# Three fused blocks on one core: another order of the chunks in the first expert pass, and another end of the last chunk

## The chip, the cores and the metric

One Trainium2 chip, one of its cores. The metric is device time in microseconds (us). The kernel before takes 1118.63 us, the median of three runs (1117.74 to 1119.43).

## The reference

```python
def _attn_ref(q, k, v, phi):            # batch 4, 8 heads, 576 positions, head 64; phi gives 32 memory slots
    a = exp(phi - max(phi, axis=2)); a = a / (sum(a, axis=2) + 1e-09)
    k_m = einsum('bhsm,bhsd->bhmd', a, k)
    v_m = einsum('bhsm,bhsd->bhmd', a, v)
    attn = softmax(q @ k_m.T / sqrt(64))
    return attn @ v_m

def _moe_ref(x, w_in, w_out):           # x 2304 x 512, w_in 512 x 2048
    h = x @ w_in
    g = h * clip(h + 3, 0, 6) / 6
    return g @ w_out

def _moe2_ref(x, domain_probs, w1, w2): # 4 experts, w1 512 x 1024 and w2 1024 x 512 each
    p = domain_probs / (domain_probs.sum(-1, keepdims=True) + 1e-09)
    out = 0
    for e in range(4):
        h = maximum(x @ w1[e], 0)
        out += p[:, e:e+1] * (h @ w2[e])
    return out
```

`reference()` runs the three blocks one behind the other, all in float32; the output is 2304 x 512.

## The kernel before, in words

The kernel has two halves, each laid out by its own planner (class `Plan`): every operation gets an engine, an estimated cost and its dependencies, the planner puts them in an order per engine, and each engine then works its list strictly in that order. TensorE's order in the second half is not the planner's: `t_order` writes it out, and `before` chains each TensorE operation to the one ahead.

The first half (up to about 394 us) does the attention, the gated block and, beside them, part of the work on the expert weights. The second half does the experts. It is cut into **three passes** over 768 tokens each (two halves of TW = 384), and each pass into **eight chunks** of 512 of the experts' 4096 inner columns: chunk n belongs to expert n // 2. A place in this sequence of 24 is called g, so g // 8 is the pass and, before the change, g % 8 the chunk.

A chunk is done with fast matrix multiplication by blocks: seven products instead of eight. At its start stand 14 product groups (`prod`, L910: seven products for each of two units u), which end in the PSUM tiles pa, pb, pd; then come 14 down groups (`down`, L979: seven results k in the order `DOWN` = 1, 5, 7, 6, 2, 4, 3, two halves j each), which end in po. Each group is six matmuls of 128x128 by 128x384, since every operand is split into a high and a low part and three of the four combinations are computed. So a chunk is 28 groups of six on TensorE, with no other work there. The products of a chunk pass through VectorE (t, s: L937, L946, L951) and are split into h (ScalarE L955 the high part, VectorE L959 the low one) for the down groups. The first two products of a chunk are put ahead of the down groups of the chunk before it (`hoist`).

The down results are summed in SBUF over the eight chunks. In the first pass nearly every po bank is **seeded**: ScalarE copies the running sum into the bank (L971), TensorE adds onto it, ScalarE copies it back (L985). Where a group is not seeded, VectorE adds po to the sum (L987). At a pass's last chunk the seven sums are combined into the four output blocks by VectorE (`total`, L990: named u2s, u3s, u4s, c2 to c5 after what they make) and stored (L995). C21 is sum 4.

**The weights.** Every chunk needs 14 weight tiles of 512 KB, called ring tiles (j = 0 to 6 for the products, 7 to 13 for the down groups), in a ring of ten slots, so a slot is free for a new tile when the tile ten back has been used for the last time. A ring tile holds the block sums that the fast multiplication wants, split into high and low parts. For chunks 0 to 4 (`NPRE` = 5) these tiles are made in the first half and stored in DRAM (`ready`). Chunks 5, 6 and 7 are **made on the spot** in the first pass: raw weights are loaded (praw, L372 and L414, three buffers), VectorE forms the sums (L393, L433), ScalarE and VectorE split them into the ring slot (L382 and L385 for the products' tiles, L422 and L425 for the down tiles), and SyncE's queue (SP) stores each tile to DRAM (L388, L428) for passes two and three. All other chunks are read from DRAM by one DMA for each tile (`ring_load`, L895). All DMAs stand in SP's one queue, in order.

The shares of the experts (share, L899: the factors p, 384 KB for one expert and pass, two buffers) are loaded once for each expert and pass.

The planner takes a VectorE operation of 384 columns as 468 ns and a ScalarE copy as 381 ns:

```python
    MM6 = 1041
    V1, A1, C1 = 468, 415, 381
    hoist = lambda g: 0 < g < NG
```

Of the kernel before, what the change touches and what calls it, by code (L numbers as in the profile page):

```python
# [22 lines left out]
E, FF2 = 4, 1024  # L23
# [14 lines left out]
NRAW, NST = 3, 6  # L38
NPRE = 5
GSEED = (0,1,2)  # L40
SEED = ((4, 0), (4, 1), (1, 0), (5, 0), (5, 1), (7, 0), (7, 1), (6, 0), (2, 0), (3, 0))
# [42 lines left out]
class Plan:  # L84
# [9 lines left out]
    def op(self, key, eng, cost, fn, *deps, banks=()):  # L94

        self.ops[key] = eng, cost, fn, deps, banks
# [64 lines left out]
def body(ctx: ExitStack, tc: tile.TileContext, phiT, kv, qT, w_in, w_out, w1, w2, dp, out):  # L161
# [719 lines left out]
    def ring_tile(g, j):  # L881
        if (g, j) not in ring:
            ring[g, j] = slot(RING[place[g, j] % len(RING)], [P, 1024], f"ring{g}_{j}")
        return ring[g, j]

    def jraw_tile(shape, name):
        t = edge_tile(len(jraws) % 3, name)
        jraws.append(t)
        a, b = shape[1:]
        return t.rearrange("p (a f) -> p a f", a=a)  # L890

    def ring_load(i):
        g, j = seq[i]
        ring_tile(g, j)
        nc.sync.dma_start(out=ring[g, j].bitcast(F32), in_=ready[g % NCE][j])  # L895

    def share_load(p, e):
        shr[p, e] = ppool.tile([P, 2, TW], F32, tag="share", name=f"share{p}_{e}")
        nc.sync.dma_start(out=shr[p, e].rearrange("p a t -> p (a t)"),  # L899
                          in_=shared[e, p * 2 * TW:(p + 1) * 2 * TW].partition_broadcast(P))  # L900
# [38 lines left out]
    def scaled(name, half, g, u):  # L939
        s = shr[divmod(g // 2, E)][:, half]  # L940
# [66 lines left out]
    for g in range(NG):  # L1007
# [20 lines left out]
    def freed(i):  # L1028
        if i < len(RING):
            return []  # L1030
        g, j = seq[i - len(RING)]
        return [("pr", g, *LAST[j]) if j < 7 else ("dn", g, DOWN[j - 7], 1), *(stored(g, j) if NPRE <= g < NCE else [])]

    def fetched(g, j, h=None):
        if not NPRE <= g < NCE:
            return [("rl", place[g, j])]
        if j >= 7:
            return [("jv", g, 2, DOWN[j - 7])]
        return [("jv", g, *x) for x, y in UP.items() if y == j and (j != 4 or x[0] == h)]

    def plan_experts():
        loads = []
        for i, (g, j) in enumerate(seq):
            if not NPRE <= g < NCE:
                deps = freed(i)
                if g >= NCE and g % NCE >= NPRE:
                    deps += stored(g % NCE, j)
                op(("rl", i), "Q", 1450, partial(ring_load, i), *loads[-1:], *deps)
                loads.append(("rl", i))
        prev, raws = [], []  # L1050
        for n in range(NPRE, NCE):

# [5 lines left out]
            def part(key, w, hi, lo, store, *deps):  # L1058
                u, k = key
                i = place[n, 7 + DOWN.index(k) if u == 2 else UP[u, k]]  # L1060
# [4 lines left out]
            prepare(n, load, part, op, partial(prep_unit, raw_tile=jraw_tile, place_tile=ring_tile),  # L1065
                    partial(prep_down, raw_tile=jraw_tile, place_tile=ring_tile), "jp", "jl", "jv")
        for p in range(NP):
            for e in range(E):
                n = p * E + e
                op(("sh", p, e), "Q", 1450, partial(share_load, p, e), *([("v", 4 * n - 5, "m12")] if n > 1 else []))  # L1070
        for g in range(NG):
            p, n = divmod(g, NCE)
            share = ("sh", *divmod(g // 2, E))
            for u in range(2):
# [30 lines left out]
            for i, k in enumerate(DOWN):  # L1105
                for j in range(2):
# [19 lines left out]
            if last:  # L1126
# [24 lines left out]

    sd, jraws = [], []
    plan_experts()
# [34 lines left out]
```

## Time and profile before

| | |
|---|---|
| median of three runs | 1118.63 us (1117.74 to 1119.43) |
| the profiled execution: its own time | 1117.6 us |
| its span, from the first to the last instruction | 1115.8 us |
| TensorE (PE) busy | 1087.0 us, 97% |
| VectorE (DVE) busy | 854.7 us, 77% |
| ScalarE (ACT) busy | 757.8 us, 68% |
| SP's DMA queue, share of the 16 DMA engines | 68.6% |

In the profile L followed by a number is a line of the kernel. A row of the timeline gives the start in us, the busy time, the engine, the line, what is written from what is read, and how many instructions are merged (x); brackets at its end give how long the engine was idle before it and who ended that. PEld is TensorE's weight load, which runs beside its matmuls. SPq is SP's DMA queue.

### The profile page before, as it was taken

The numbers are of one execution on the slowest core, as the hardware profiler recorded it, in microseconds if no ns is written. First come the engines' busy times: TensorE is split into PE (matmuls) and PEld (weight loads), VectorE is DVE, ScalarE is ACT, GpSimd is POOL, SyncE is SP. The second block draws the span as 40 slices with busy tenths as digits, with TensorE's granted clock in tenths as the row PEclk, the third lists the DMA queues.
The fourth block names the chain that finished last, engine by engine and source line by source line (L and its number), as shares of the span: only waits on it lengthen the run. The fifth ranks groups of instructions, "written<-read, shape, count | busy, mean of one in ns | idle before, by whom it ended". The sixth has DMA issues, their size and how long they took to land.

```text
span 1115.8 us, 18432 instructions
## 1 busy us (share of the span) xinstructions
PE 1087.0 (97%) x6777; PEld 1054.3 (94%) x6777; DVE 854.7 (77%) x1709; ACT 757.8 (68%) x1600; POOL 1.2 (0%) x8
## 2 busy tenths in 40 slices
PE   6999999999999999999999999999999999999997
PEld 4799989999999999999999889999999999999997
DVE  6999999997888565555899997666666966666668
ACT  2666768677777556777998746666667566666664
POOL 0000000000000000000000000000000000000000
PEclk9999999999999999999999999999999999999999
DMA  9844436557897068767678787767677977776673
GB/s 359 301 163 134 142 107 240 171 197 296 301 330 288 13 239 284 263 246 264 239 279 296 275 308 270 265 243 262 248 263 254 332 267 278 258 262 250 248 260 113
DMA packets 80153, 273.64 MB, mean 245 GB/s; under 512 B 8824, under 2 KB 11968, under 8 KB 79552
## 3 DMA queue, kind: packets, MB, share of 16 engines
q1 hardware_dynamic: 80064, 272.48, 68.6%
q8 instruction: 53, 0.87, 0.3%
q14 instruction: 36, 0.29, 0.1%
HBM read 208.97 MB, written 63.48 MB: 244 GB/s over the span
## 4 chain that ended last, share of the span: by engine, by line
PE 83%; DVE 7%; ACT 6%; issue 2%; DMA 2%; SPq 0%; DVEq 0%; ACTq 0%
PE po L979 24%; PE pacc L741 18%; PE pb L910 11%; PE ph L712 10%; PE pa L910 8%; PE pd L910 7%; PE psc L540 2%; PE pu L695 2%; ACT po L971 2%; DVE h L959 1%; DVE t L946 1%; ACT sum L985 1%; ACT h L955 1%; DMA out_y<-sum 1%; ACT ring L382 1%
## 5 line engine op out<-in xcount | busy, mean ns | idle before, releaser
L979 PE MATMUL po<-h,ring 128*128 128x384 f32 x2016 | 359.6, 337 | 6.6 <-ACT sum L985 2.3
L979 PEld LDWEIGHTS po<-h,ring 128*128 128x128 f32 x2016 | 352.2, 189 | 10.1 <-ACT sum L985 2.6
L741 PE MATMUL pacc<-g,w 128*128 128x384 f32 x1152 | 219.2, 337 | 1.4 <-ACT pacc L748 1.4
L741 PEld LDWEIGHTS pacc<-g,w 128*128 128x128 f32 x1152 | 198.9, 188 | 13.0 <-issue 10.1
L959 DVE TENSOR_TENSOR h<-t,h 128x384 fp32r<-128x384 f32 x288 | 153.0, 553 | 41.9 <-ACT h L955 41.2
L955 ACT CAST h<-t 128x384 fp32r<-128x384 f32 x288 | 144.7, 514 | 58.4 <-DVE t L951 35.3
L910 PE MATMUL pb<-xop,ring 128*128 128x384 f32 x864 | 173.7, 335 | 0.3 <-ACT u L933 0.2
L910 PEld LDWEIGHTS pb<-xop,ring 128*128 128x128 f32 x864 | 151.6, 188 | 1.7 <-ACT u L933 1.7
L712 PE MATMUL ph<-attnT,u 128*128 128x384 f32 (+1 forms) x768 | 124.6, 304 | 0.0
L910 PE MATMUL pa<-xop,ring 128*128 128x384 f32 x576 | 116.1, 335 | 1.4 <-DVE ring L385 0.7
L937 DVE TENSOR_TENSOR t<-pd,u 128x384 f32<-128x384 f32 x96 | 53.2, 554 | 82.7 <-ACT u L933 82.7
L910 PE MATMUL pd<-xop,ring 128*128 128x384 f32 x576 | 115.3, 334 | 0.0
L712 PEld LDWEIGHTS ph<-attnT,u 128*128 128x128 f32 x768 | 114.3, 189 | 0.5 <-DVE attnT L454 0.2
L910 PEld LDWEIGHTS pa<-xop,ring 128*128 128x128 f32 x576 | 101.0, 188 | 2.7 <-DVE ring L385 1.3
L910 PEld LDWEIGHTS pd<-xop,ring 128*128 128x128 f32 x576 | 101.3, 188 | 0.0
L718 ACT ACTIVATE t<-ph,three 128x384 f32<-128x384 f32 x96 | 55.7, 582 | 46.7 <-PE ph L712 42.3
L933 ACT COPY u<-pb 128x384 f32<-128x384 f32 x96 | 46.0, 479 | 55.0 <-PE pb L910 52.0
L985 ACT COPY sum<-po 128x384 f32<-128x384 f32 x130 | 61.9, 478 | 12.0 <-PE po L979 5.4
L451 ACT CAST g<-t 128x384 fp32r<-128x384 f32 x96 | 49.5, 515 | 28.7 <-PE pacc L741 27.9
L722 DVE SCALAR_TENSOR_TENSOR t<-t,ph 128x384 f32<-128x384 f32 x96 | 52.6, 549 | 17.8 <-ACT t L718 17.3
L971 ACT COPY po<-sum 128x384 f32<-128x384 f32 x112 | 54.2, 484 | 13.2 <-DVE sum_b L987 7.7
L454 DVE TENSOR_TENSOR g<-t,g 128x384 fp32r<-128x384 f32 x96 | 52.9, 552 | 7.5 <-ACT g L451 6.9
(107 smaller groups left out, 1164.0 us busy)
## 6 DMA issues: line engine op xcount, KB each, us to landing
ring<-ready SPq DMA_DIRECT2D x294, 512.0 KB, 5.2
ready<-ring SPq DMA_DIRECT2D x39, 512.0 KB, 5.1
ready<-B SPq DMA_DIRECT2D x35, 512.0 KB, 4.7
praw<-in_w SPq DMA_DIRECT2D x32, 512.0 KB, 4.9
ready<-W SPq DMA_DIRECT2D x30, 512.0 KB, 3.4
raw<-in_w_in SPq DMA_DIRECT2D x16, 512.0 KB, 4.6
kv<-in_kv SPq DMA_DIRECT2D x16, 512.0 KB, 9.3
raw<-in_w_out SPq DMA_DIRECT2D x16, 512.0 KB, 3.4
```

The source lines that it names most:

```text
L454: nc.vector.tensor_tensor(out=lo, in0=src, in1=hi.bitcast(F32), op=ALU.subtract)
L712: nc.tensor.matmul(ps[:, o:o + m], uts[c, b][:, x, hq, i * P:(i + 1) * P], attnT[b][:, y, hq, s0:s0 + m], start=(k == 0), stop=(k == 5))
L718: nc.scalar.activation(t, st["ph", n], AF.Relu, bias=three, scale=1.0)
L722: nc.vector.scalar_tensor_tensor(out=t, in0=t, scalar=6.0, in1=st.pop(("ph", n)), op0=ALU.min, op1=ALU.mult)
L741: nc.tensor.matmul(pacc[j][:, 0:TW], w[:, x, j * P:(j + 1) * P], g[:, y], start=(i == 0 and k == 0 and not more), stop=(i == NI - 1 and k ...
L910: nc.tensor.matmul(bks[b, g, u], w[:, xx, kt * P:(kt + 1) * P], xop[x][:, y, kt], start=first and kt == 0 and n == 0, stop=kt == 1 and n == 2,
L937: nc.vector.tensor_tensor(out=tmp_tile(name, g, u), in0=bks["d", g, u], in1=y, op=ALU.add)
L955: nc.scalar.copy(h[:, 0], tmp[name, u])
L959: nc.vector.tensor_tensor(out=h[:, 1], in0=tmp[name, u], in1=h[:, 0].bitcast(F32), op=ALU.subtract)
L971: nc.scalar.copy(down_bank(g, k, j), sums[k][:, j])
L979: nc.tensor.matmul(ps, w[:, x, u, j * P:(j + 1) * P], hts[k, u][:, y], start=u == 0 and n == 0 and not more, stop=u == 1 and n == 2, skip_ ...
L985: nc.scalar.copy(o, ps)
```

## The change

`FIRST` sets the order of the chunks in the first pass: 0, 1, 5, 2, 6, 3, 7, 4. So the three chunks that are made on the spot stand at the third, fifth and seventh place instead of the sixth to eighth, and the pass ends with a chunk that is read. Passes two and three keep 0 to 7. Shares are now loaded whenever the expert changes from one place to the next: seven loads in the first pass, where it was four.

In every pass's last chunk C21's sum (k = 4) is no longer seeded: its total c4 is made from the sum so far, ahead of the last chunk's part, and VectorE then adds the two halves of that part from PSUM; in the last pass its halves are stored one by one. The outputs are stored in the order 5, 2, 4, 3 (before: 4, 5, 2, 3).

In the very last chunk TensorE's order of the last products is another one, and the first down group comes between other products than before.

```diff
 NPRE = 5
+FIRST = (0, 1, 5, 2, 6, 3, 7, 4)
...
+    def chunk(g):
+        return FIRST[g] if g < NCE else g % NCE
+
     def ring_load(i):
         g, j = seq[i]
-        ring_tile(g, j)
-        nc.sync.dma_start(out=ring[g, j].bitcast(F32), in_=ready[g % NCE][j])
...
+        nc.sync.dma_start(out=ring_tile(g, j).bitcast(F32), in_=ready[chunk(g)][j])
...
     def seeded(g, k, j):
         n = g % NCE
-        return n > 0 and not (n == NCE - 1 and k in (2, 3)) and (g < NCE or (k, j) in SEED)
+        return n > 0 and not (n == NCE - 1 and k in (2, 3, 4)) and (g < NCE or (k, j) in SEED)
...
             a, b = t_order[-14], t_order[-13]
-            t_order[-16:-12] = [a, one(1, 5), b, one(1, 6)]
+            t_order[-20:-12] = [one(1, 0), one(0, 6), one(1, 2), one(1, 3), one(1, 5), a, one(1, 6), b]
...
-        return [("pr", g, *LAST[j]) if j < 7 else ("dn", g, DOWN[j - 7], 1), *(stored(g, j) if NPRE <= g < NCE else [])]
+        return [("pr", g, *LAST[j]) if j < 7 else ("dn", g, DOWN[j - 7], 1), *(stored(chunk(g), j) if late_made(g) else [])]
+
+    def late_made(g):
+        return g < NCE and FIRST[g] >= NPRE
...
-        for n in range(NPRE, NCE):
+        for n in [n for n in FIRST if n >= NPRE]:
...
+        for g in range(NG):
+            p, e = g // NCE, chunk(g) // (NCE // E)
+            if g % NCE == 0 or e != chunk(g - 1) // (NCE // E):
+                new = len(shares_at)
+                shares_at.append(g)
+                op(("sh", new), "Q", 1450, partial(share_load, new, p, e),
+                   *([("v", 2 * shares_at[-2] - 1, "m12")] if new > 1 else []))
+            share_of[g] = new
...
-                    if last and k == 2:
-                        deps.append(("c2", p))
-                    if last and k == 3:
-                        deps.append(("c3", p))
+                    if last and k in (2, 3, 4):
+                        deps.append((f"c{k}", p))
...
-                op(("c4", p), "V", 868, t(4, 4, 7), ("u3s", p), *ev(4))
-                for k, *d in ((4, ("c4", p)), (5, ("c5", p)), (2, *ev(2)), (3, *ev(3))):
-                    if k in (2, 3) and p == NP - 1:
+                op(("c4", p), "V", 868, t(4, 4, 7), ("u3s", p), *prev_(4))
+                for k, *d in ((5, ("c5", p)), (2, *ev(2)), (4, *ev(4)), (3, *ev(3))):
+                    if k in (2, 3, 4) and p == NP - 1:
```

In the lists below, ring5_10 is tile 10 of place 5 (before the last number, which only counts tiles), praw5_3 the fourth raw load of chunk 5, ready2 the stored tiles of chunk 2, h6_5_1 the h for k = 6 of place 5 and unit 1. The line numbers of the changed kernel are up to 13 higher.

VectorE, where the down groups of the first made chunk begin. Before, this is place 5:

```order
L959 TENSOR_TENSOR h2_5_1_6671<-t12_5_1_6607,h2_5_1_6671 128x384
L951 TENSOR_TENSOR t22_5_0_6465<-t12_5_0_6510,t11_5_0_6303 128x384
L951 TENSOR_TENSOR t22_5_1_6556<-t12_5_1_6607,t11_5_1_6495 128x384
L946 SCALAR_TENSOR_TENSOR t11_6_0_6699<-pa_6549,share0_3_6035 128x384
L425 TENSOR_TENSOR ring5_12_6694<-praw5_3_6422,ring5_12_6694 128x512
L385 TENSOR_TENSOR ring6_4_6707<-praw6_0_6463,ring6_4_6707 128x256
L393 TENSOR_TENSOR praw6_0_6463<-praw6_0_6463 128x256 x3
L959 TENSOR_TENSOR h3_5_0_6732<-t22_5_0_6465,h3_5_0_6732 128x384
L959 TENSOR_TENSOR h3_5_1_6735<-t22_5_1_6556,h3_5_1_6735 128x384
```

In the changed kernel the same chunk stands at place 2:

```order
L965 TENSOR_TENSOR h2_2_1_5701<-t12_2_1_5664,h2_2_1_5701 128x384
L957 TENSOR_TENSOR t22_2_0_5485<-t12_2_0_5531,t11_2_0_5323 128x384
L426 TENSOR_TENSOR ring2_12_5717<-praw5_3_5439,ring2_12_5717 128x512
L957 TENSOR_TENSOR t22_2_1_5584<-t12_2_1_5664,t11_2_1_5516 128x384
L952 SCALAR_TENSOR_TENSOR t11_3_0_5741<-pa_5564,share2_5306 128x384
L965 TENSOR_TENSOR h3_2_0_5746<-t22_2_0_5485,h3_2_0_5746 128x384
L965 TENSOR_TENSOR h3_2_1_5754<-t22_2_1_5584,h3_2_1_5754 128x384
L965 TENSOR_TENSOR h1_3_0_5780<-t11_3_0_5741,h1_3_0_5780 128x384
L386 TENSOR_TENSOR ring4_0_5790<-praw6_0_5560,ring4_0_5790 128x2x256
```

What moved: before, the last tile of chunk 5 (ring5_12) is followed at once by the first part and the sums of chunk 6 (ring6_4, praw6_0); now the last tile (ring2_12) is followed by the work of place 3, whose weights are read; of the next made chunk only the first tile (ring4_0) stands near it.

SP's queue, where a made chunk hands over to a chunk that is read. Before, there is one such place in the program, from place 7 (chunk 7) to place 8 (chunk 0 of the second pass):

```order
L428 DMA ready7_117<-ring7_9_7314 128x1024
L895 DMA ring8_5_7418<-ready0_110 128x1024
L895 DMA ring8_6_7427<-ready0_110 128x1024
L428 DMA ready7_117<-ring7_10_7394 128x1024
L895 DMA ring9_0_7459<-ready1_111 128x1024
L428 DMA ready7_117<-ring7_11_7276 128x1024
L895 DMA ring8_7_7492<-ready0_110 128x1024
L428 DMA ready7_117<-ring7_12_7456 128x1024
L895 DMA ring8_8_7512<-ready0_110 128x1024
L428 DMA ready7_117<-ring7_13_7354 128x1024
L995 DMA out_y<-sum_a_4727 128x2x384
```

Now there are three; this is the first, from place 2 (chunk 5) to place 3 (chunk 2):

```order
L429 DMA ready5_115<-ring2_9_5550 128x1024
L901 DMA ring3_1_5598<-ready2_112 128x1024
L901 DMA ring3_2_5613<-ready2_112 128x1024
L901 DMA ring3_3_5634<-ready2_112 128x1024
L901 DMA ring3_4_5651<-ready2_112 128x1024
L429 DMA ready5_115<-ring2_11_5536 128x1024
L901 DMA ring3_5_5688<-ready2_112 128x1024
L901 DMA ring3_6_5704<-ready2_112 128x1024
L429 DMA ready5_115<-ring2_10_5662 128x1024
L429 DMA ready5_115<-ring2_12_5717 128x1024
L901 DMA ring3_7_5758<-ready2_112 128x1024
L901 DMA ring3_8_5778<-ready2_112 128x1024
```

What moved: the same pattern, in which a load stands behind a store and can start only when the tile ten back has been stored, now stands at places 3, 5 and 7.

TensorE at the last chunk (place 23), from the seventh product group on. Before:

```order
L910 MATMUL pd_12426<-xop6_4448,ring23_4_12326 128x384 x6
L910 MATMUL pb_12458<-xop4_4423,ring23_5_12348 128x384 x6
L910 MATMUL pd_12503<-xop5_4439,ring23_6_12362 128x384 x6
L910 MATMUL pb_12458<-xop3_4411,ring23_6_12362 128x384 x6
L979 MATMUL po_12394<-h1_23_0_12339,ring23_7_12376 128x384 x3
L979 MATMUL po_12394<-h1_23_1_12494,ring23_7_12376 128x384 x3
L910 MATMUL pb_12458<-xop2_4401,ring23_5_12348 128x384 x6
L979 MATMUL po_12549<-h1_23_0_12339,ring23_7_12376 128x384 x3
L979 MATMUL po_12549<-h1_23_1_12494,ring23_7_12376 128x384 x3
L910 MATMUL pd_12503<-xop6_4448,ring23_4_12326 128x384 x6
L979 MATMUL po_12413<-h5_23_0_12485,ring23_8_12392 128x384 x3
```

And now:

```order
L916 MATMUL pb_12460<-xop4_4423,ring23_5_12350 128x384 x6
L916 MATMUL pd_12428<-xop6_4448,ring23_4_12328 128x384 x6
L916 MATMUL pb_12460<-xop3_4411,ring23_6_12364 128x384 x6
L916 MATMUL pd_12514<-xop5_4439,ring23_6_12364 128x384 x6
L916 MATMUL pb_12460<-xop2_4401,ring23_5_12350 128x384 x6
L985 MATMUL po_12396<-h1_23_0_12341,ring23_7_12378 128x384 x3
L985 MATMUL po_12396<-h1_23_1_12499,ring23_7_12378 128x384 x3
L916 MATMUL pd_12514<-xop6_4448,ring23_4_12328 128x384 x6
L985 MATMUL po_12563<-h1_23_0_12341,ring23_7_12378 128x384 x3
L985 MATMUL po_12563<-h1_23_1_12499,ring23_7_12378 128x384 x3
L985 MATMUL po_12415<-h5_23_0_12487,ring23_8_12394 128x384 x3
```

What moved: unit 1's products (the second pb and pd) stand earlier, the last of its pb groups one group earlier, ahead of both down groups of k = 1 (ring23_7).

VectorE's last rows of the program. Before:

```order
L990 TENSOR_TENSOR sum6_4730<-sum6_4730,sum5_4729 128x768
L990 TENSOR_TENSOR sum_b_4728<-sum_b_4728,sum6_4730 128x768
L990 TENSOR_TENSOR sum_b_4728<-sum_b_4728,sum7_4731 128x768
L990 TENSOR_TENSOR sum5_4729<-sum5_4729,sum7_4731 128x768
L987 TENSOR_TENSOR sum_b_4728<-po_12681,sum_b_4728 128x384
L987 TENSOR_TENSOR sum_b_4728<-po_12690,sum_b_4728 128x384
```

And now:

```order
L996 TENSOR_TENSOR sum_b_4728<-sum_b_4728,sum6_4730 128x768
L996 TENSOR_TENSOR sum5_4729<-sum5_4729,sum7_4731 128x768
L993 TENSOR_TENSOR sum_b_4728<-po_12680,sum_b_4728 128x384
L993 TENSOR_TENSOR sum_b_4728<-po_12688,sum_b_4728 128x384
L993 TENSOR_TENSOR sum_b_4728<-po_12661,sum_b_4728 128x384
L993 TENSOR_TENSOR sum_b_4728<-po_12670,sum_b_4728 128x384
```

What moved: both totals into sum_b (c3 and c4) stand ahead of what po brings, and four additions from po stand behind the last total instead of two.

## Rows read from the trace of the kernel before

**Rows 1.** Timeline of PE, second half: where chunks 0, 4, 5, 6, 8 and 9 begin their down groups.

```profile
412.08 8.13 PE L979 MATMUL po<-h,ring 128*128 128x384 f32 x46
...
529.10 14.72 PE L979 MATMUL po<-h,ring 128*128 128x384 f32 x84
...
555.27 0.97 PE L910 MATMUL pa<-xop,ring 128*128 128x384 f32 x4 [0.39 <-DVE ring L385]
...
559.20 1.03 PE L979 MATMUL po<-h,ring 128*128 128x384 f32 x5
...
591.16 12.65 PE L979 MATMUL po<-h,ring 128*128 128x384 f32 x72
...
636.84 4.37 PE L979 MATMUL po<-h,ring 128*128 128x384 f32 x12 [1.88 <-DVE sum_a L987]
...
655.63 6.59 PE L979 MATMUL po<-h,ring 128*128 128x384 f32 x36
664.53 10.15 PE L979 MATMUL po<-h,ring 128*128 128x384 f32 x48 [2.31 <-ACT sum L985]
...
689.08 11.08 PE L979 MATMUL po<-h,ring 128*128 128x384 f32 x63
```

**Rows 2.** Timeline of all engines: the same place of chunks 15 and 16.

```profile
863.83 14.72 PE L979 MATMUL po<-h,ring 128*128 128x384 f32 x84
...
892.95 12.29 PE L979 MATMUL po<-h,ring 128*128 128x384 f32 x70
```

**Rows 3.** Windows of one chunk's length: busy us of each engine, clock, DMA share, GB/s.

```profile
452.60:481.80 29.20, 29.20 (x171) 29.20 (x170) 16.70 (x34) 21.99 (x50) 0.00 (x0) 1.00 0.75 267
...
540.00:569.10 29.10, 28.71 (x165) 28.02 (x164) 27.37 (x56) 25.36 (x57) 0.00 (x0) 1.00 0.76 274
569.10:598.20 29.10, 27.59 (x153) 26.07 (x152) 28.37 (x59) 25.54 (x57) 0.00 (x0) 1.00 0.85 311
```

**Rows 4.** Windows of 5 us around the two long waits of PE.

```profile
635.00:640.00 5.00, 3.08 (x9) 2.38 (x10) 5.00 (x9) 2.72 (x5) 0.00 (x0) 0.75 0.62 169
...
665.00:670.00 5.00, 5.00 (x21) 5.00 (x21) 3.92 (x7) 3.32 (x9) 0.00 (x0) 0.67 1.03 420
```

**Rows 5.** Lines of VectorE, 394 to 690 us: all preparation of chunks 5 to 7.

```profile
L385 DVE TENSOR_TENSOR ring<-praw,ring 128x512 fp32r<-128x512 f32 (+1 forms) x24 | 14.7, 621 | 6.1 <-ACT ring L382 6.0
L425 DVE TENSOR_TENSOR ring<-praw,ring 128x512 fp32r<-128x512 f32 x21 | 14.4, 686 | 0.2 <-ACT ring L422 0.2
L393 DVE TENSOR_TENSOR praw<-praw 128x256 f32<-128x256 f32 x24 | 10.1, 422 | 0.4
L433 DVE TENSOR_TENSOR praw<-praw 128x512 f32<-128x512 f32 x6 | 4.1, 687 | 0.0
L433 DVE TENSOR_TENSOR praw<-praw,praw 128x512 f32<-128x512 f32 x6 | 4.1, 685 | 0.0
```

**Rows 6.** Timeline of all engines at the two ends of a pass.

```profile
655.39 0.54 SPq L995 DMA_DIRECT2D out_y<-sum  x1
...
664.00 0.86 ACT L985 COPY sum<-po 128x384 f32<-128x384 f32 x2 [2.33 <-DMA out_y<-sum]
...
884.35 0.39 SPq L995 DMA_DIRECT2D out_y<-sum  x1
...
893.88 0.55 DVE L959 TENSOR_TENSOR h<-s,h 128x384 fp32r<-128x384 f32 x1
```

**Rows 7.** Timeline of SP: a load behind the last made chunk.

```profile
652.12 0.32 SPq L895 DMA_DIRECT2D ring<-ready  x1
```

**Rows 8.** Waits of SP's own queue: us in total, times, longest.

```profile
SPq L895 <- DMA ready<-ring: 23.6, 6, 4.7
```

**Rows 9.** DMA issues by kind: count, KB, median us to landing.

```profile
ready<-ring SPq DMA_DIRECT2D x39, 512.0 KB, 5.1
```

**Rows 10.** Timeline of all engines at the end of the program.

```profile
1098.32 12.08 PE L979 MATMUL po<-h,ring 128*128 128x384 f32 x68 [0.68 <-DVE h L959]
...
1111.13 1.02 DVE L987 TENSOR_TENSOR sum_b<-po,sum_b 128x384 f32<-128x384 f32 x2
```

More of the change, by code (lines that the diff above doesn't have):

```diff
@@ L884, in ring_tile, with made_tile @@
         return ring[g, j]
+    def made_tile(n, j):
+        return ring_tile(FIRST.index(n), j)
     def jraw_tile(shape, name):
@@ L890, in jraw_tile, with share_load @@
         return t.rearrange("p (a f) -> p a f", a=a)
+    def chunk(g):
+        return FIRST[g] if g < NCE else g % NCE
     def ring_load(i):
         g, j = seq[i]
-        ring_tile(g, j)
-        nc.sync.dma_start(out=ring[g, j].bitcast(F32), in_=ready[g % NCE][j])
-    def share_load(p, e):
-        shr[p, e] = ppool.tile([P, 2, TW], F32, tag="share", name=f"share{p}_{e}")
-        nc.sync.dma_start(out=shr[p, e].rearrange("p a t -> p (a t)"),
+        nc.sync.dma_start(out=ring_tile(g, j).bitcast(F32), in_=ready[chunk(g)][j])
+    def share_load(k, p, e):
+        shr[k] = ppool.tile([P, 2, TW], F32, tag="share", name=f"share{k}")
+        nc.sync.dma_start(out=shr[k].rearrange("p a t -> p (a t)"),
                           in_=shared[e, p * 2 * TW:(p + 1) * 2 * TW].partition_broadcast(P))
@@ L939, in scaled @@
     def scaled(name, half, g, u):
-        s = shr[divmod(g // 2, E)][:, half]
+        s = shr[share_of[g]][:, half]
         if name in ("t11", "t21"):
@@ L1031, in freed @@
         g, j = seq[i - len(RING)]
-        return [("pr", g, *LAST[j]) if j < 7 else ("dn", g, DOWN[j - 7], 1), *(stored(g, j) if NPRE <= g < NCE else [])]
+        return [("pr", g, *LAST[j]) if j < 7 else ("dn", g, DOWN[j - 7], 1), *(stored(chunk(g), j) if late_made(g) else [])]
+    def late_made(g):
+        return g < NCE and FIRST[g] >= NPRE
     def fetched(g, j, h=None):
-        if not NPRE <= g < NCE:
+        if not late_made(g):
             return [("rl", place[g, j])]
+        n = chunk(g)
         if j >= 7:
-            return [("jv", g, 2, DOWN[j - 7])]
-        return [("jv", g, *x) for x, y in UP.items() if y == j and (j != 4 or x[0] == h)]
+            return [("jv", n, 2, DOWN[j - 7])]
+        return [("jv", n, *x) for x, y in UP.items() if y == j and (j != 4 or x[0] == h)]
     def plan_experts():
@@ L1043, in plan_experts @@
         for i, (g, j) in enumerate(seq):
-            if not NPRE <= g < NCE:
+            if not late_made(g):
                 deps = freed(i)
-                if g >= NCE and g % NCE >= NPRE:
-                    deps += stored(g % NCE, j)
+                if g >= NCE and chunk(g) >= NPRE:
+                    deps += stored(chunk(g), j)
                 op(("rl", i), "Q", 1450, partial(ring_load, i), *loads[-1:], *deps)
@@ L1059, in part @@
                 u, k = key
-                i = place[n, 7 + DOWN.index(k) if u == 2 else UP[u, k]]
+                i = place[FIRST.index(n), 7 + DOWN.index(k) if u == 2 else UP[u, k]]
                 op(("jh", n, *key), "A", 92 + w / 1.2, hi, *deps, *freed(i))
@@ L1063, in part @@
                 op(("js", n, *key), "Q", 1450 if w == 512 else 800, store, ("jv", n, *key))
[L1065 to L1070, printed above, removed]
+            prepare(n, load, part, op, partial(prep_unit, raw_tile=jraw_tile, place_tile=made_tile),
+                    partial(prep_down, raw_tile=jraw_tile, place_tile=made_tile), "jp", "jl", "jv")
+        for g in range(NG):
[6 more added lines that the diff above has]
+            share_of[g] = new
         for g in range(NG):
             p, n = divmod(g, NCE)
-            share = ("sh", *divmod(g // 2, E))
+            share = ("sh", share_of[g])
             for u in range(2):
@@ L1150, in plan_experts @@
                         op(key, e2, cost, fn, *deps)
-    sd, jraws = [], []
+    sd, jraws, share_of, shares_at = [], [], {}, []
     plan_experts()
```

## The prediction

> **What bounds the kernel now.** I read the timeline of TensorE (PE) first. PE does 28 groups in a chunk whatever the others do, so the distance between the starts of two chunks' down groups tells what was lost. Undisturbed it is 892.95 - 863.83 = 29.12 us [rows 2]. From chunk 0 (412.08) to chunk 9 (689.08) it should be nine times that, 262.08 us, and is 277.00: **14.92 us are lost in the first pass and at its end** [rows 1]. By pieces: up to chunk 4 0.54, chunk 4 to 5 0.98, 5 to 6 2.84, 6 to 8 6.23, 8 to 9 4.33 [rows 1]. Up to the start of chunk 4's down groups all weights that PE used were read from DRAM; the loss grows as chunks 5, 6, 7 are made.
>
> The windows say why. In a chunk without preparation VectorE is busy for 16.70 of 29.2 us; while chunks 5 and 6 are made it is busy for 27.37 and 28.37 of 29.1, so it is full [rows 3]. PE's two longest waits, 1.88 and 2.31 us, come at the end of this stretch, the first for a VectorE addition, the second for ScalarE's copy of a down result [rows 1]. That copy itself waited 2.33 us for the store of an output sum, which was issued only at 655.39; in the next pass the same store, at 884.35, is issued 8.60 us ahead of the start of the next down groups (892.95), where here it is 0.24 us ahead (655.63) [rows 1, 2, 6]. So VectorE's lateness reaches PE directly and through the totals. Around each of the two waits PE's granted clock is below full, 0.75 and 0.67 over 5 us; that is about 1.25 and 1.65 us more, from stretches at 1.2 instead of 2.4 GHz, and lies within the 14.92 [rows 4].
>
> **The change, part by part.** The sum is made against the profiled execution's own 1117.6 us (span 1115.8); the median of the runs shown is 1.0 us above it.
>
> *Spreading the made chunks.* Preparation costs VectorE 14.7 + 14.4 + 10.1 + 4.1 + 4.1 = 47.4 us for three chunks, 15.8 for one [rows 5]. With the chunk's own 16.7 that is 32.5 in 29.1 us: 3.4 too much for each chunk, and three in a row add up to 10.2. Now a chunk that is read lies behind each: 2 x 16.7 + 15.8 = 49.2 us of work in 58.2, so the lag can be worked off before the next begins. The work itself is the same and no PE group is added or removed: minus 14.9.
>
> What a made chunk costs by itself remains. Its cost is read from the first one before, which had nothing late ahead of it: 0.54 + 0.98, less the 0.39 that PE waited at 555.27 for a VectorE tile; by the order that tile is the first of chunk 6, in whose place there is now a read tile [rows 1]. That is 1.13, three times 3.4. The first made chunk now follows chunk 0, whose down groups aren't seeded, so ScalarE has less to do there and I drop 0.5: **plus 2.9**. Bounds: 0, if each has the room that the sum of work says, and three times 0.54 + 0.98 + 2.84 = 4.36, 13.1 in all, if an isolated chunk pays all that was paid from chunk 4 to chunk 6. I stay near the low end, because from chunk 5 to 6 two chunks' preparation overlapped, which no longer happens.
>
> *Transfers.* Raw loads, stores and reads are the same in number; three share loads of 384 KB are added. A share load waits for the last use of the share before last, and stands about a chunk (29 us) ahead of its use: 0. Behind that wait in SP's queue stand stores of made tiles and the read of the next chunk's first tile; they have a chunk's down groups, 14 us, as cover, and if it were gone each microsecond would count. The hand-over from a made to a read chunk happens three times instead of once. There a read waits until the tile ten back is stored: 23.6 us in six waits, 4.7 at most [rows 8]. But the tightest read that I find there, issued at 652.12, holds the third down result's weights and is wanted four groups of 29.12 / 28 = 1.04 us into the next down groups (655.63 + 4 x 1.04 = 659.8), and reads and stores take about 5.1 us [rows 1, 7, 9]: some 2.5 us to spare, in a stretch in which everything was late. 0; its failure is a rival.
>
> One rule of the Trainium skill speaks against this part. The page "DMA: Bandwidth & Descriptors", section "Latency and other measured facts", says that the confirmation of a write dominates a DMA's fixed cost, slowest for HBM, and grows from 0.2 to 2 us under load. By it the estimate would be up to 1.8 us more for a store at each hand-over, still inside the 2.5, so the sum would be the same. The row has the stores at 5.1 us in a loaded stretch, and that decides [rows 9].
>
> *The ends of the passes.* At each pass's end C21 now costs VectorE two additions more, 1.02 us [rows 10], and ScalarE four copies less. At the second pass's end VectorE is late but just in time: the split that the second down result needs ends at 893.88 + 0.55 = 894.43, and PE wants it after two and a half groups of 1.04, at 895.55 [rows 2, 6]. 1.12 to spare against 1.02. I take 0.15 for each of two pass ends: **plus 0.3**; bounds 0 and 4.33, if the end of the first pass goes as it does now.
>
> *The end of the program.* PE waits 0.68 us at 1098.32 for a split by VectorE [rows 10]. The product on which that split hangs now stands one group (1.04 us) earlier; VectorE's list ahead of it is as long as before, so I take half: minus 0.5. Behind the last total stand four additions instead of two, and VectorE works without a pause there: plus 1.0. **Plus 0.5** in all; bounds minus 0.7 (wait gone, additions hidden) and plus 1.0.
>
> Sum: 1117.6 - 14.9 + 2.9 + 0.3 + 0.5 = 1106.4, and with the 1.0 between this execution and the median **1107.4 us**; I say 1107.
>
> **Rivals.** (a) *A made chunk pays 2.84 each time, what was lost from chunk 5 to 6.* For it: in its down groups ScalarE copies the running sum into each bank and out again, group by group, and every tile that it splits between them makes the next bank late; spreading doesn't change that. Against it: fewer splits fall into these groups, as only one made chunk is under way. 3 x 2.84 = 8.5 instead of 2.9: 1113.0.
>
> (b) *The first pass's end keeps its loss of 4.33.* For it: more VectorE work there, and chunk 7 is finished only one chunk ahead. Against it: the second pass's end has the same totals and loses nothing. 1107.4 - 0.15 + 4.33 = 1111.6.
>
> (c) *Slower: the hand-over.* If the reads of chunks 2, 3 and 4 land late because each stands behind stores that wait for VectorE, PE waits at three places. It decides at (14.9 - 0.3 - 0.5) / 3 = 4.7 us for each hand-over, that is at reads 2.5 + 4.7 = 7.2 us later than the one at 652.12 was. With two stores' landing more, 10.2 us, it would be 7.7 and a clock stretch of 1.65 each: 28 us instead of 2.9, 1132.5. Against it: at the one hand-over before no wait of PE names a DMA. The skill's rule above belongs here: by it the spare time shrinks to 0.7 us, and the chance is a little higher than the rows alone would make it.
>
> (d) *No change:* the first pass's loss comes from something else than preparation in a row, and 13 us of it stay (the upper bound above): 1117.6.
>
> **How the numbers follow.** Forecast 0.63, (a) 0.17, (b) 0.12, (c) 0.04, (d) 0.04. A measurement of this kernel tells 0.2%, some 2.2 us, from no change. Forecast, (a) and (b) are all faster by more: 0.92; same 0.04; slower 0.04. The forecast's own range comes from its bounds: 1107.4 - 2.9 - 0.3 - 1.2 = 1103.0 at the low end, half the way to (a), 1110.2, at the high one. To leave out no more than 2 in 10 the range takes in (a) and (b): 1103 to 1113.5.
>
> **What the profile after would show.** Right: the distance from the first chunk's down groups to the tenth's near 262.08 + 3; VectorE's windows in the first pass all near 22 to 27 us, none full over two chunks; no wait of PE above 1.5 us in it, and the clock at 1.00 there; the store of output 5 at the first pass's end issued several us ahead of the next down groups; the stretch behind PE's last matmul longer by 0.5 to 1 us. Wrong: waits of PE on ScalarE's seeds in the down groups of places 2, 4, 6 (a), on output stores at the first pass's end (b), or on reads of ring tiles (c).

## The result: 1105.1 us, and the profile after

The changed kernel takes **1105.09 us** (median; 1104.29 to 1105.29), beside 1119.03 us for the kernel before on the same chip: ratio 0.9872, 95% interval 0.9855 to 0.989. The medians are 13.9 us apart. The profiled execution took 1105.05 us, with a span of 1103.3 (before: 1117.6 and 1115.8).

Line numbers have moved by one, from 890 on by six: L895 is now L901, L979 is L985, L987 is L993, L990 is L996, L995 is L1001. "Place" is the position of a chunk in the first pass; the made chunks 5, 6, 7 stand in the places 2, 4, 6, and before in 5, 6, 7. First PE's timeline, where the chunks in the places 0, 2, 6, 7 and the first two of the next pass begin their down groups:

```profile
412.60 14.72 PE L985 MATMUL po<-h,ring 128*128 128x384 f32 x84
...
471.27 14.72 PE L985 MATMUL po<-h,ring 128*128 128x384 f32 x84
...
588.78 14.72 PE L985 MATMUL po<-h,ring 128*128 128x384 f32 x84
618.15 14.72 PE L985 MATMUL po<-h,ring 128*128 128x384 f32 x84
647.27 14.72 PE L985 MATMUL po<-h,ring 128*128 128x384 f32 x84
676.39 14.72 PE L985 MATMUL po<-h,ring 128*128 128x384 f32 x84
```

676.39 - 412.60 is 263.79 instead of 277.00 us [rows 1]: 1.71 over nine times 29.12 is left of 14.92. From place 6 to 7 it is 0.25, and both steps of the pass's end are 29.12, so nothing is lost there. In the windows the clock is 1.00 throughout; three of the first pass, each one chunk long (PE, PEld, VectorE, ScalarE, GpSimd, clock, DMA share, GB/s):

```profile
452.60:481.70 29.10, 29.08 (x168) 28.58 (x167) 26.81 (x54) 26.08 (x58) 0.00 (x0) 1.00 0.90 308
481.70:510.80 29.10, 29.10 (x169) 28.99 (x168) 20.17 (x41) 23.81 (x55) 0.00 (x0) 1.00 0.81 291
...
598.10:627.20 29.10, 29.10 (x169) 28.82 (x168) 25.00 (x46) 26.34 (x56) 0.00 (x0) 1.00 0.75 261
```

Up to place 6 VectorE alternates between 27 and 20 us a chunk, where it had two full chunks in a row [rows 3]. The timeline of all engines at the pass's end has two rows that matter below. VectorE's first difference for the next pass's inputs starts 19.46 us ahead of the last chunk's down groups (618.15), and the store of output 5 is issued 6.63 us ahead of the next pass's (647.27), where before it was 0.24 [rows 1, 6]:

```profile
598.69 0.95 DVE L799 TENSOR_TENSOR xe<-acc,acc 128x768 f32<-128x768 f32 x1
...
640.64 0.39 SPq L1001 DMA_DIRECT2D out_y<-sum  x1
```

SP's queue waits longer for stores of made tiles than before [rows 8], and no wait of PE comes of it:

```profile
SPq L901 <- DMA ready<-ring: 33.2, 7, 6.2
```

At the end of the program PE's wait of 0.68 us [rows 10] is gone, and VectorE ends with four additions instead of two:

```profile
1083.06 14.05 PE L985 MATMUL po<-h,ring 128*128 128x384 f32 x78
...
1097.71 1.94 DVE L993 TENSOR_TENSOR sum_b<-po,sum_b 128x384 f32<-128x384 f32 x4
```

PE is done at 1097.11, 6.19 us before the span's end; before it was 1098.32 + 12.08 = 1110.40, 5.40 before it [rows 10].

### The profile page after: what moved, and what is told of

Its sections match the earlier page's. It is cut to its first block, busy times and chain, and to the rows that moved or that the text cites. A ratio compares the mean times of both kernels' runs of the same rounds, so it can differ in the third digit from the quotient of the medians.

```text
span 1103.3 us, 18433 instructions
## 1 busy us (share of the span) xinstructions
PE 1080.5 (98%) x6777; PEld 1051.0 (95%) x6777; DVE 857.4 (78%) x1715; ACT 752.0 (68%) x1588; POOL 1.2 (0%) x8
## 4 chain that ended last, share of the span: by engine, by line
PE 95%; DVE 2%; DMA 1%; issue 1%; ACT 0%; DVEq 0%; SPq 0%; ACTq 0%
PE po L985 30%; PE pacc L742 19%; PE pb L916 14%; PE ph L713 10%; PE pa L916 9%; PE pd L916 9%; PE psc L541 2%; PE pu L696 2%; DMA raw<-in_w_in 0%; PE pk L515 0%; DMA kv<-in_kv 0%; DVE h L965 0%; PE pe L586 0%; DVE sum L996 0%; PE pa L498 0%
## 5 line engine op out<-in xcount | busy, mean ns | idle before, releaser
L985 PE MATMUL po<-h,ring 128*128 128x384 f32 x2016 | 353.8, 334 | 0.1
L985 PEld LDWEIGHTS po<-h,ring 128*128 128x128 f32 x2016 | 349.8, 188 | 0.4 <-DVE h L965 0.4
```

Of the source, the lines that this page charges most:

```text
L985: nc.tensor.matmul(ps, w[:, x, u, j * P:(j + 1) * P], hts[k, u][:, y], start=u == 0 and n == 0 and not more, stop=u == 1 and n == 2, skip_ ...
```

## The experiments

The theory on record (**a**) says that VectorE has 3.4 us too much in each made chunk, that three in a row add up, and that a read chunk behind each lets it catch up. The rivals grew with the runs: **b**, ScalarE's copies in the down groups; **c**, the hand-over from made to read tiles; and, found in the trace after, **d**, the next pass's inputs. Their differences are written into the buffers of the last raw tiles (`edge_tile`), so they can't start before the last made chunk is split. In the old order that is in the middle of the last chunk's down groups (from 633.06 us).

One table serves all runs. A loss is the distance between the starts of down groups in PE's timeline, less 29.12 us a chunk, as in the prediction: in the **middle** from place 0 to 7, at **end 1** from place 7 to the next pass's first chunk, at **end 2** to its second. The kernel before was timed with each set of four: 1118.53, 1118.81 and 1119.12 us. The losses come from one profiled execution of each kernel, whose time lies up to 1.5 us off the median (E5 1118.05 us, E1 1106.24). The middle repeats well: E2 has the order of before and 5.41, E1 the new order and 1.77.

| kernel | us (median) | ratio to before, 95% | middle | end 1 | end 2 |
|---|---|---|---|---|---|
| before | 1119.03 | | 5.44 | 5.15 | 4.33 |
| after | 1105.09 | 0.9855 to 0.989 | 1.71 | 0 | 0 |
| E1 order only | 1104.86 | 0.9856 to 0.9901 | 1.77 | 0.03 | 0 |
| E2 rest only | 1116.70 | 0.9971 to 0.9994 | 5.41 | 5.82 | 2.50 |
| E3 three early | 1112.72 | 0.9928 to 0.9965 | 9.55 | 0 | 0 |
| E4 before, no sums | 1118.09 | 0.9979 to 1.0007 | 5.04 | 3.92 | 6.00 |
| E5 made last | 1116.57 | 0.9962 to 0.9987 | 2.34 | 3.40 | 8.04 |
| E6 inputs late | 1108.73 | 0.9883 to 0.9924 | 1.66 | 2.67 | 0 |
| E7 copies on GpSimd | 1121.93 | 1.0017 to 1.0045 | 10.80 | 7.43 | 1.09 |
| E8 before, ten seeds | 1116.55 | 0.9958 to 0.9986 | 2.77 | 5.12 | 6.71 |
| E9 splits twice | 1124.93 | 1.0042 to 1.0067 | 21.26 | 0 | 0 |
| E10 copies twice | 1129.54 | 1.0081 to 1.0106 | 26.17 | 0 | 0 |
| E11 after, ten seeds | 1104.21 | 0.9855 to 0.9888 | 0.28 | 0 | 0 |
| E12 two in a row | 1117.78 | 0.998 to 1.0005 | 13.78 | 0 | 0 |

**E1 and E2: which part of the change.** E1 takes back the sum of C21 and the last chunk's order; E2 takes back the order of the first pass:

```diff
-FIRST = (0, 1, 5, 2, 6, 3, 7, 4)
+FIRST = (0, 1, 2, 3, 4, 5, 6, 7)
```

> The kernel before with the new order of the first pass alone; C21's sum and the last chunk's order are as before. Theory (the order carries the gain, the rest nets nothing): within 1 us of the changed kernel, 1104.5 to 1106.1, and the ten down groups of the first pass 263 to 265 us apart. Rival (the first pass's end needs the new sum of C21 to lose nothing): 4.33 us of the old loss come back at the pass's end, 1109.4.

> The changed kernel with the chunks in the old order: only C21's sum and the last chunk's order are changed. Theory: the time of the kernel before, 1117.5 to 1119.5, with some 15 us lost in the first pass. Rival (the store of output 4 and the copies that go away at the pass's end carry part of the gain): the 4.33 us of the pass's end are saved, 1114.7.

E1 is as fast as the whole change, as its theory said, and loses 0.03 at the pass's end. E2 gains 1.8 us, a little more than its theory allowed and less than its rival: C21's new sum, with the stores in the new order, saves 1.83 at end 2 and gives 0.67 back at end 1. With the new order of the chunks it is worth nothing.

**E3: three in a row, but early.**

```diff
-FIRST = (0, 1, 5, 2, 6, 3, 7, 4)
+FIRST = (0, 1, 5, 6, 7, 2, 3, 4)
```

> The changed kernel with the three made chunks in a row again, but early: 0, 1, 5, 6, 7, 2, 3, 4. Theory (three in a row overload VectorE, wherever they stand): 14.92 - 4.33 = 10.6 us are lost instead of 1.7, and the pass's end loses nothing, since three read chunks lie between: 1105.1 + 8.9 = 1114.0, range 1111 to 1116. Rival (what costs is that they stand at the end of the pass, ahead of its totals): as the changed kernel, 1105 to 1107. Rival (all 15 us come back, wherever the row stands): 1118.3.

9.55 us are lost, near the 10.6 of the theory, whose range the time meets, and none at the pass's end. The second of the row costs 2.84, as in the old order. But 3.73 of them fall in the first read chunk's down groups behind the row (from 563.88 to the next, 596.73). PE's two longest waits of the stretch (us in total, times, longest) stand there and name ScalarE and a read, which in the chain of waits follows a store of 5.05 us:

```profile
PE po L985 <- ACT h L961: 1.7, 1, 1.7
PE po L985 <- DMA ring<-ready: 1.5, 1, 1.5
```

So a row costs something wherever it stands; this run doesn't yet say for which engine.

**E4: VectorE relieved in the old order.** Eight such operations, of which one is shown, are left out for the made chunks:

```diff
-        op(z(1), "V", 336, st["s1"], y(3))
+        op(z(1), "V", 336, st["s1"] if pp != "jp" else (lambda: None), y(3))
```

> The kernel before, in its old order, without the eight sums and differences that VectorE makes in the raw tiles of each chunk prepared on the spot (chunks 5, 6, 7 get wrong weights); ScalarE's copies, the splits, the stores and the loads all stay. Theory (VectorE is overloaded): 47.4 - 29.1 us are left, 9.7 a chunk, with the chunk's own 16.7 that is 26.4 in 29.1 us, so the row no longer adds up: at least 10 of the 14.9 us come back, 1105 to 1109. Rival (the transfers or ScalarE are what is late): no change beyond 2 us, 1116 to 1119.

The time stays the same, far from the theory's 10 us: theory a falls here. In the middle 0.40 of the 5.44 us come back, where PE's wait of 0.39 at 555.27 is gone; the two ends together lose 9.92 instead of 9.48, and are taken up below. The step from place 5 to 6 stays (2.84 and 2.88). The windows over place 5's down groups show why, first of before, then of E4:

```profile
559.20:573.90 14.70, 14.00 (x79) 13.34 (x78) 14.28 (x30) 14.09 (x33) 0.00 (x0) 1.00 0.67 233
```

```profile
559.20:573.90 14.70, 13.98 (x79) 13.32 (x77) 11.32 (x23) 14.11 (x33) 0.00 (x0) 1.00 0.70 250
```

VectorE went from 14.28 to 11.32 us, PE lost the same 0.7, and ScalarE stayed at 14.1. Its timeline in E4 has no wait there behind 559.57; each down group brings a copy out (sum<-po) and one in (po<-sum), and the copies of made tiles (ring<-praw) and of h stand between them:

```profile
566.35 0.48 ACT L971 COPY po<-sum_a 128x384 f32<-128x384 f32 x1
566.77 0.47 ACT L985 COPY sum<-po 128x384 f32<-128x384 f32 x1
567.14 0.62 ACT L422 CAST ring<-praw 128x512 fp32r<-128x512 f32 x1
567.66 0.49 ACT L971 COPY po<-sum_a 128x384 f32<-128x384 f32 x1
568.07 0.41 ACT L382 CAST ring<-praw 128x256 fp32r<-128x256 f32 x1
568.38 0.48 ACT L985 COPY sum<-po 128x384 f32<-128x384 f32 x1
```

PE's waits in the down groups of places 5 and 6, 1.3 us in three, name such a copy (po, L971), in before as in E4. Place 5's down groups take 1.65 us of the 2.84 (E4: 1.68). The rest falls among the products of place 6, where PE waits for the split of a made tile (L385); that stays too, with VectorE at 15.12 of 17.26 us in E4:

```profile
573.90:591.16 17.26, 16.41 (x90) 15.63 (x91) 15.12 (x30) 14.18 (x31) 0.00 (x0) 1.00 0.97 366
```

That ScalarE is full doesn't prove it the cause either. In place 4's down groups of before it is as full, and PE loses nothing:

```profile
529.10:543.80 14.70, 14.70 (x86) 14.70 (x86) 10.97 (x25) 14.20 (x33) 0.00 (x0) 1.00 0.29 110
```

The runs that relieve ScalarE have to decide.

**E7 and E8: ScalarE relieved in the old order.** E7 gives the copies of made tiles to GpSimd; E8 seeds ten of the 14 down results:

```diff
-        return n > 0 and not (n == NCE - 1 and k in (2, 3)) and (g < NCE or (k, j) in SEED)
+        return n > 0 and not (n == NCE - 1 and k in (2, 3)) and (k, j) in SEED
```

> The kernel before, in its old order, with ScalarE's 45 copies into the made tiles given to GpSimd, which is idle there; VectorE's list is the same. ScalarE loses 8.7 us of work in each made chunk. Theory (b: ScalarE, which copies sums in and out of the banks in the down groups, is what is late while chunks are made in a row): the 4 to 5 us lost up to the last chunk's down groups come back and the pass's end stays as it is, 1113 to 1115.5. Theory (a: VectorE): no change, 1117.5 to 1119.5. If a GpSimd copy takes more than about 1.5 us, the made tiles themselves come late and the time is above 1120, which would tell nothing between the two.

> The kernel before, with the first pass's down results seeded as in the later passes: 10 of 14 instead of all. In each chunk ScalarE loses eight copies (3.9 us), and VectorE gains four additions (2.2 us). Theory b (ScalarE): 2 to 4 us come back, 1114.5 to 1116.5. Theory a (VectorE's sum of work): 2.2 us more in each of three full chunks, 1123 to 1125.

E7 is above 1120 and tells nothing between the two: made tiles come late (PE waits 4.2 us in three for their splits), since a GpSimd copy takes 991 ns where ScalarE's of the same shape took 620. The 1.5 us that the expectation named as the limit were too generous. The row of GpSimd (busy us, mean ns):

```profile
L422 POOL CAST ring<-praw 128x512 fp32r<-128x512 f32 x21 | 20.8, 991 | 44.0 <-DVE praw L433 23.5 <-PE pd L910 16.1 <-PE pb L910 2.6
```

E8 halves the loss in the middle, 5.44 to 2.77, although VectorE gets more to do. Its window over place 5's down groups has VectorE without a pause and PE too:

```profile
557.90:572.60 14.70, 14.70 (x87) 14.70 (x86) 14.70 (x33) 13.86 (x32) 0.00 (x0) 1.00 0.73 249
```

So in the middle it is ScalarE (b) that has to be relieved first. VectorE comes next: PE's waits that are left in the middle, 1.4 us in two, name its splits of made tiles (L385). At the ends E8 loses 11.83 instead of 9.48. End 1 is as before (5.12); all of the rise is at end 2.

**E5 and E6: the end of the pass.** E5 puts the same spaced order one place later; E6 holds the next pass's inputs back in the changed kernel:

```diff
-FIRST = (0, 1, 5, 2, 6, 3, 7, 4)
+FIRST = (0, 1, 2, 5, 3, 6, 4, 7)
```

```diff
-deps += [("xlo", p, key[2])] if p else [x for r in raws[-NRAW:] for x in r]
+deps += [("xlo", p, key[2])] if p else [x for r in raws[-NRAW:] for x in r] + [("dn", 7, 4, 0)]
```

> The changed kernel with the made chunks one place later each: 0, 1, 2, 5, 3, 6, 4, 7. They stand apart as in the changed kernel, but the last of them ends the pass. Theory on record (VectorE's sum of work): apart they cost nothing, 1105 to 1106.5. New theory (the differences for the next pass's inputs stand in the buffers of the last raw tiles, so they start only when the last made chunk is split, and then crowd the pass's end): 4 to 8 us are lost from the last chunk's down groups to the next pass's, 1109 to 1113.

> The changed kernel, with one wait more: the differences for the second pass's inputs (VectorE's four subtractions into the raw buffers) may not start before the eleventh of the last chunk's 14 down results, where they stand in the kernel before; nothing else is changed. New theory (their lateness is the larger half of the old loss): the pass's end loses 4 to 8 us again, 1109 to 1113. Rival (the pass's end was slow because made chunks stood in front of it): at most 1 us, 1105 to 1106.

E5 loses almost all of the gain, 11.44 us at the two ends, with nothing in a row. That misses both theories: end 1 loses 3.40, less than the new theory's 4 to 8, and 8.04 fall one chunk later, at end 2, which it didn't name. E6 loses 2.67 again at end 1, between its theory and its rival. The windows from place 7's down groups to the next pass's say how these sizes come about; after, E6, E5 and before:

```profile
618.20:647.30 29.10, 29.10 (x170) 29.10 (x169) 29.08 (x52) 14.86 (x33) 0.00 (x0) 1.00 1.00 382
```

```profile
617.70:649.50 31.80, 29.68 (x170) 29.10 (x170) 31.51 (x55) 17.28 (x36) 0.00 (x0) 1.00 0.90 348
```

```profile
619.20:651.70 32.50, 30.39 (x169) 28.97 (x168) 32.50 (x55) 18.19 (x37) 0.00 (x0) 1.00 0.70 220
```

```profile
621.40:655.60 34.20, 31.88 (x169) 30.20 (x168) 34.00 (x58) 20.17 (x43) 0.00 (x0) 0.95 0.74 242
```

VectorE is full in all four, with totals, splits and the next inputs. After is among them, and there PE loses nothing, so here too it is PE's waits that name the engine. Before, the longest is for VectorE's addition to sum_a, 1.88 us [rows 1]; E5 has the same wait, and E6 one for the next inputs (xop); first E5, then E6:

```profile
PE po L985 <- DVE sum_a L993: 2.1, 2, 1.4
```

```profile
PE pb L916 <- DVE xop L796: 1.3, 1, 1.3
```

The change took work out of the stretch. Before, four differences of 0.95 us stand in it (after: one), and the splits and differences of the last made chunk; E6 puts three differences back, 2.85 us of work, and loses 2.67. By lines of VectorE in E5's stretch, the made chunk's part is 4.1 us, and the loss 3.40:

```profile
L426 DVE TENSOR_TENSOR ring<-praw,ring 128x512 fp32r<-128x512 f32 x4 | 2.7, 683 | 0.0
...
L434 DVE TENSOR_TENSOR praw<-praw 128x512 f32<-128x512 f32 x1 | 0.7, 683 | 0.0
L434 DVE TENSOR_TENSOR praw<-praw,praw 128x512 f32<-128x512 f32 x1 | 0.7, 682 | 0.0
```

E4 agrees at end 1. It leaves out the two operations of the second kind, the addition to sum_a starts 0.69 us earlier (635.45, before 636.14), and the loss is 3.92 instead of 5.15. Part of that may be the clock, 1.00 in E4's stretch:

```profile
621.40:654.40 33.00, 30.17 (x169) 28.95 (x168) 32.31 (x55) 19.88 (x42) 0.00 (x0) 1.00 0.75 235
```

End 2 goes with the store of output 5. Issued 6.63 us (after) and 6.48 us (E6) ahead of the next pass's down groups, it costs nothing; 0.34 ahead (E2, with the clock at 1.00 there) end 2 loses 2.50, 0.24 ahead (before, 0.95) 4.33, and behind them, by 1.08 (E4), 1.06 (E8) and 2.44 (E5), 6.00, 6.71 and 8.04. What makes the store late is not VectorE alone. Before, its total is done at 653.88 and the store is issued 1.51 us later [rows 6]. In E4 the total is done 1.00 earlier, and the store still goes out at 655.49; first before, then E4, VectorE and SP:

```profile
652.93 0.95 DVE L990 TENSOR_TENSOR sum<-sum,sum 128x768 f32<-128x768 f32 x1
```

```profile
651.93 0.95 DVE L990 TENSOR_TENSOR sum<-sum,sum 128x768 f32<-128x768 f32 x1
```

```profile
652.69 0.32 SPq L895 DMA_DIRECT2D ring<-ready  x1
653.06 0.42 SPq L899 DMA_DIRECT2D share<-shared  x1
653.54 1.41 SPq L895 DMA_DIRECT2D ring<-ready  x3
655.06 0.39 SPq L995 DMA_DIRECT2D out_y<-sum_b  x1
655.49 0.81 SPq L995 DMA_DIRECT2D out_y<-sum  x1
```

The store stands in SP's queue behind reads for the next pass, and SP itself waits for stores of made tiles ahead of these reads (18.1 us in four waits between 636 and 662 us). It is the hand-over of rival c, met through an output store. In E2 and after, the store follows its total within 0.1 us.

**E9 and E10: how much room a made chunk has when spread.**

```diff
-op(("jv", n, *key), "V", 72 + w / 0.97, lo, ("jh", n, *key))
+op(("jv", n, *key), "V", 72 + w / 0.97, lambda: (lo(), lo()), ("jh", n, *key))
```

E10 does the same with the copy (`hi`).

> The changed kernel, with VectorE's 15 splits of each chunk made on the spot done twice (the second writes the same numbers again): 9.6 us more VectorE work in each of the three. Record's arithmetic (two chunks' time takes what two chunks and one preparation need): 49.2 + 9.6 = 58.8 in 58.2 us, so it only begins to cost, 1105.5 to 1108. Theory N (a made tile's buffer comes free only some ten tiles ahead of its use, so the work has to be done in about one chunk's time, where VectorE is busy 26.8 of 29.1 us already): about 7 us for each made chunk, less what can be put off, 1115 to 1127.

> The changed kernel, with ScalarE's 15 copies of each chunk made on the spot done twice: 8.7 us more ScalarE work in each of the three. Theory b (ScalarE in the down groups is what a made chunk presses on; it is busy 26.1 and 23.8 us of each two chunks, 49.9 + 8.7 = 58.6 in 58.2): each made chunk pays at least the 2.84 us that the second of a row paid, 1113.5 to 1130. Theory a (VectorE alone sets what a made chunk costs): 1105 to 1107.

Neither engine has room for the work twice, ScalarE the less: 19.55 us more for 28.9 us of splits, 24.46 for 26.2 of copies (in part the clock, 0.88 from 455.80 to 470.50 in E10). Both times lie in the ranges of theory N and theory b. For VectorE the record's arithmetic, 58.8 in 58.2 us, fails: by places E9 loses 4.84 to 4.87 on the way into each made chunk. Its window over the products ahead of the first one has VectorE at 14.46 of 14.7 and PE at 11.61. PE's waits name ScalarE's copy u (8.8 us in six), but ScalarE is busy for only 9.40 there and waits for VectorE's t:

```profile
457.00:471.70 14.70, 11.61 (x63) 10.34 (x62) 14.46 (x29) 9.40 (x21) 0.00 (x0) 1.00 0.73 268
```

**E11: ScalarE relieved in the new order.**

```diff
-... (g < NCE or (k, j) in SEED)
+... (g < NCE and not 2 <= g <= 6 or (k, j) in SEED)
```

> The changed kernel, with 10 of 14 down results seeded by ScalarE in the places 2 to 6 of the first pass, as in the later passes; the other four are added by VectorE (ScalarE 3.9 us less, VectorE 2.2 us more a chunk; the last place keeps its seeds). Theory b (what is left of a made chunk's cost is ScalarE's): 1 to 1.6 of the 1.7 us still lost in the first pass come back, 1103.5 to 1104.2. Theory a (VectorE): 26.8 + 2.2 us in 29.1, no gain, 1105 to 1107.

The loss in the first pass falls from 1.71 to 0.28 us, so what was left of a made chunk's cost was mostly ScalarE's as well. The median is 0.9 us below the changed kernel's, in another set of runs; the intervals overlap, so the gain is shown by the trace and not by the times. It has the lowest median of this study.

**E12: two in a row.**

```diff
-FIRST = (0, 1, 5, 2, 6, 3, 7, 4)
+FIRST = (0, 1, 5, 6, 2, 7, 3, 4)
```

> The changed kernel with two made chunks in a row and the third apart: 0, 1, 5, 6, 2, 7, 3, 4. Theory (the second of a row pays 2.84 us for ScalarE's copies, and the hand-over from a row to a read chunk a little, since its reads stand behind the stores): 1108 to 1110. Rival (only three in a row, or the end of the pass, cost anything): 1105 to 1106.

Neither: 13.78 us are lost. The second of the row costs 2.43, as the theory said, but 9.30 fall between the starts of down groups in places 4 and 5. ScalarE's copy for a tile of chunk 7 waits 8.68 us for a store, and with it stand the seeds behind it in its queue. Its timeline, VectorE's and SP's, and PE's wait:

```profile
542.27 0.62 ACT L383 CAST ring<-praw 128x512 fp32r<-128x512 f32 x1 [8.68 <-DMA ready<-ring]
```

```profile
519.12 0.69 DVE L386 TENSOR_TENSOR ring<-praw,ring 128x512 fp32r<-128x512 f32 x1 [0.89 <-ACT ring L383]
```

```profile
532.88 0.53 SPq L389 DMA_DIRECT2D ready<-ring  x1
```

```profile
PE po L985 <- ACT po L977: 6.7, 2, 6.5
```

By the order of the program the store is that of chunk 7's own first tile, whose buffer a later tile of the same chunk takes. That tile was split by 519.81, and its store was issued 13.07 us later; of the nine issues ahead of it in SP's queue six are reads of chunk 2 and two are stores of chunk 6, which are late themselves behind the row. It is rival c's place, with ScalarE as the one that is held up.

## Why the forecast came true, and where its reasons didn't

The span fell by 12.5 us. Worked out by the prediction's steps: 14.92 - 1.71 = 13.21 came back in the first pass and its end; the end of the program got 0.19 longer (from the down groups ahead of the last ones at 1067.67 and 1054.98 to the span's end, 48.13 and 48.32); the second half began 0.52 later (412.60, not 412.08), which nothing in the change explains. The forecast of 1107 was 1.9 us too high. Of the 2.3 us between its sum, 1107.4, and the median, 1.3 come from the terms below and the later start; the other 1.0 is the distance between profiled execution and median, which was 1.0 before and 0.04 after.

**"VectorE is full and three in a row add up to 10.2" failed**, although the loss it was to explain did go. In the middle, 5.44 of the 14.92 us, the engine that sets PE's pace is ScalarE, with the copies of made tiles between those of the sums: shown by E4 (VectorE relieved by 6.1 us a chunk, 0.40 back), E8 and E11 (ScalarE relieved, 2.67 and 1.43 back). A full engine in a window was taken for the bound; the row of before had ScalarE at 25.4 us in the same window [rows 3], and it was full only in the down groups.

**"VectorE's lateness reaches PE directly and through the totals" holds for half of the end, and not for a sum over three chunks.** The other 9.48 us belong to the pass's end. End 1, 5.15, is VectorE's: the last made chunk's splits, the totals and the next pass's inputs meet there, the inputs late because their buffers are the raw tiles'. End 2, 4.33, is the store of output 5, which the prediction put down to a late total; the total was 1.51 us ahead of it, and an earlier one in E4 did not move it. SP's queue, with reads behind the stores of made tiles, has its part, and how large it is was not measured. E5 shows that the last place alone brings 11.44 us, E6 that late inputs alone bring 2.67. The clock's part, 2.9 us by the prediction's estimate, came back too: 0.95 in end 1's window of before, 1.00 in that of after, and 1.00 at end 2:

```profile
647.27:676.39 29.12, 29.12 (x169) 29.12 (x169) 21.59 (x44) 18.29 (x40) 0.00 (x0) 1.00 0.70 254
```

That the term of minus 14.9 came out is in part luck. It put two losses with different causes into one, and the new order, with its apart chunks and a read chunk at the end, happens to remove both.

**"A read chunk behind each made one lets the lag be worked off" is too coarse.** E9 fits another view: the work of a made chunk must be done between the release of its buffers and its use, in about one chunk's time. No run varied the release itself. The new order fits because single chunks do (26.8 us of VectorE in 29.1), and it has little to spare.

**What three made chunks cost**, 2.9, measured 1.71, and **the pass ends**, 0.3, measured 0: both mis-sized within their bounds. 1.31 of the 1.71 come on the way into the made chunks (0.43 to 0.45 each). **The end of the program**, 0.5, measured 0.19: PE's part got 0.60 shorter (42.73 to 42.13 us), the wait of 0.68 wholly gone rather than halved, and the rest 0.79 longer.

**The rivals.** (a), that ScalarE's copies make each made chunk dear, had the right engine and the wrong size: an isolated chunk pays 0.5 to 0.7, a second in a row 2.4 to 2.9. (b) did not come: the store of output 5 went out 6.63 us early. (c) did not come here, and E3 and E12 show it as real in two other orders. In the old order it had a part in end 2. Against it the prediction held that at the one hand-over before no wait of PE names a DMA; but ScalarE's copy waited 2.33 us for the output store behind it [rows 6], and PE for that copy.

Left open: how E3's 3.73 us behind the row divide between reads and ScalarE, what end 2 would be with the output store ahead of the reads, and whether another order of SP's queue would make E12's order as good as the changed one. None of it was tried.

## What to carry to other kernels

A full engine in a window is a suspect only; leave out some of its work before a sum is built on it. Here VectorE was full and not the first limit, and ScalarE was as full in a stretch that cost nothing as in one that did. When an output is late, look whether its last operation or its place in the DMA queue is what is late. When steps are moved, look for what waits on a buffer of theirs: where the last prepared chunk stood decided when the next pass's inputs could start, which no line of the change names. Order experiments with the same work (one place later, two in a row) are cheap and show most.

## What the runs showed of the hardware

The same 128x512 copy with conversion took 991 ns on GpSimd and 620 ns on ScalarE. A store of a made tile, 5.1 us in the median of before [rows 9], took 9.32 us from issue in E12, from 532.88 to the end of the wait for it at 542.20; ScalarE and then PE stood for most of it. The 384 KB store of output 5 in before took 8.58 us, from 655.39 to 663.98, in a stretch in which the queue moved 407 GB/s (window 660 to 665); the median of its kind is 2.4 us after. The Trainium skill ("DMA: Bandwidth & Descriptors", "Latency and other measured facts") has the confirmation of a write grow to 2 us under load; 9.32 is 4.2 us over the median, and no run here shows how much of that is the confirmation.
